# Linear attention and an MLP on one core: two more parts of GEMM 2 as seven products, and a new planned order of all instructions

## The chip, the cores and the metric

The kernel runs on one core of one Trainium2 chip. The metric is the device time of one execution in microseconds (us); three runs of the kernel before are shown as their median and their two ends. One further execution was taken by the hardware profiler. Its engines are named as the profile names them: PE (TensorE, matrix products), PEld (PE's loads of the stationary operand), DVE (VectorE), ACT (ScalarE), POOL (GpSimd) and SP (SyncE, which here issues nearly all DMA transfers).

## What is computed

```python
# q, k, v: (8, 8, 576, 64); omega: (128, 64); w_in: (512, 2048); w_out: (2048, 512)
def phi(x):                         # x already divided by 64 ** 0.25
    proj = einsum('bhsd,md->bhsm', x, omega)
    h = proj - sum(x * x, -1, keepdims=True) / 2
    return exp(h - max(h, -1, keepdims=True)) / sqrt(128)
kv = einsum('bhsm,bhsd->bhmd', phi(k), v);  z = sum(phi(k), axis=2)
x = einsum('bhsm,bhmd->bhsd', phi(q), kv) / (einsum('bhsm,bhm->bhs', phi(q), z) + 1e-6)
x = x.transpose(0, 2, 1, 3).reshape(4608, 512)
h = x @ w_in                        # GEMM 1
g = h * erf(softplus(h))
out = g @ w_out                     # GEMM 2
```

## The kernel before, in words

**Attention.** The 64 pairs of batch and head are worked off as 32 pairs of heads (`attention`, numbered 0_0 to 7_3 by batch and pair of heads). A pair goes through PE five times: `ppk` and `ppq` project keys and queries, `kvp` makes keys times values, `pt` turns the query features, and `nd` makes numerator and denominator. Between these steps DVE takes maxima, ACT takes exponentials and logarithms, and DVE divides (`xs`).

**The MLP.** The 4608 tokens are six groups: two of 2 x 288 tokens (groups 0 and 1), then four of 2 x 432 (`SUPERS`). The 2048 hidden features are four parts q of 512. Per group and part, GEMM 1 fills `hs`, `chain` applies softplus, erf and the product with h (`gs`, then `hs` again), and GEMM 2 adds the part into the output tiles `os`. All numbers are split into a high and a low part in a reduced format (names that end in h and l: `xh`, `xl`, `gh`, `gl`, `bh`, `bl`, `th`, `tl`; for weights both parts lie in a tile `w` or `wb`), and each product of two tiles takes three matmuls: high by high, high by low, low by high.

**Eight products or seven.** In the plain form (`plain1`, `gemm2`) a 2 x 2 block of tiles takes eight products. In the other form (`gemm1`, `gemm2_blocks`, by the table `PRODUCTS`, Winograd's variant of Strassen's method) it takes seven, on sums of weight blocks (made by `make_sums`: tiles `R`, then `S`, then their split `c`, stored to DRAM as `wdc` and fetched again as `wb`) and on sums of the right side (`xc` for GEMM 1, `gsum` in `pieces2` for GEMM 2). In the profile, matmuls of the plain form write tiles `h` and `o`; those of the seven products write `hX`, `hY`, `hZ` and `oX`, `oY`, `oZ`. `blocked(b, q)` decides for GEMM 2: with `FIRST2 = (3, 3, 3, 3)` groups 0 to 2 are plain in all four parts, groups 3 to 5 are in seven products, but for the very last part. The sums of a part's W2 are made where group `FIRST2[q] - 1` reads its plain weights, so all in group 2. GEMM 1 is in seven products from group 2 on; its sums (W1) are made in group 1. For a group of 432 and one part, GEMM 2 takes 4 output tiles x 2 halves x 4 x 3 = 96 matmuls in the plain form and 2 x 7 x 2 x 3 = 84 in the other.

**What sets the order.** `build` writes down operations with tiles they read and write, a due time (`plan`), and the engines that may do each, with a cost (`COST`, tuples such as `("V", 0.68, -1e9)`). `Plan.order` then plays the list through once on the host: due times are pulled forward along dependences, and at each step an idle engine takes the operation with the earliest due time whose inputs and buffers are there (`LAG` after the producer's end). What comes out is one fixed order per engine; on the chip every engine works off its own list in that order and waits on semaphores. `AHEAD` is how long before its due time a weight fetch may be issued by SP. Buffers are slots per pool (`SLOTS`: 8 for weights, 11 for the `g` pool that holds `hs`, `gs`, `gh`, `gl`, `R` and `S`, 8 PSUM banks) with limits per stream (`CAPS`: one `R` and one `S` at a time). All instructions are issued through one helper, so the profile shows one line, L1008, for nearly all of them, and groups are told apart by tiles.

Of the kernel before, what the change touches and what calls it, by code (L numbers as in the profile page):

```python
# [20 lines left out]
B, H, S, D = 8, 8, 576, 64  # L21
# [41 lines left out]
            ("Y", "S4", "B22", (0, 1), 1),  # L63
            ("X", "A22", "T4", (1, 0), 0))

FIRST2 = (3, 3, 3, 3)


def blocked(b, q):

    return FIRST2[q] <= b < len(SUPERS) - (q == NQ - 1)


COST = dict(mm=0.132, proj=0.222, half=0.156, tr=0.109, kv=1.35, table=1.3)
BANDWIDTH = 270e3
LAG = {"T": 0.35, "A": 0.25, "V": 0.25, "G": 0.3, "S": 0.3}
SLOTS = dict(w=8, g=11, u=2, f=2, mx=3, sq=3, v=1, qh=1, ql=1, kh=1, kl=1, xs=12, xh=2, xl=2,
             os=4, ps=8)
CAPS = dict(st=3, wt=1, ws=1, wp=2, cv=2, att=4, moe1=5, moe2=3, hs=4, gs=2, w=6, wsums=7)
# [26 lines left out]
class Plan:  # L106
# [43 lines left out]
    def order(self, slots, caps):  # L150
        ops = self.ops
# [5 lines left out]
        for o in reversed(ops):  # L157
            due = o.plan if o.plan is not None else math.inf
            dur = min(c for _, c, _ in o.opts)
            for s in o.succ:  # L160
                due = min(due, s.due - dur - 0.4)
            o.due = due
        free = {p: list(range(n)) for p, n in slots.items()}
        held = {s: 0 for s in self.streams}
        nxt = {s: 0 for s in self.streams}
# [16 lines left out]
        def event(t, kind, x):  # L182
            nonlocal count
            count += 1
            heapq.heappush(events, (t, count, kind, x))
# [22 lines left out]
        while True:  # L208
            progress = True
            while progress:  # L210
                progress = False
                for e in engines:
# [3 lines left out]
                    while ready[e]:  # L216
                        item = heapq.heappop(ready[e])
                        o = item[2]
# [22 lines left out]
                    o = chosen  # L241
# [41 lines left out]
            while True:  # L283
                if kind == "idle":
                    idle[x] = True
                elif kind == "done":
                    for s in x.succ:
                        s.left -= 1
                        lag = 0.0 if x.eng != "S" and len(s.opts) == 1 and s.opts[0][0] == x.eng \
                            else LAG[x.eng]  # L290
                        s.ready = max(getattr(s, "ready", 0.0) if s.left >= 0 else 0.0, now + lag) \
                            if hasattr(s, "ready") else now + lag
                        if not s.left:
                            event(max(now, s.ready), "push", s)
                    event(now + LAG[x.eng], "free", x)
                elif kind == "free":
# [19 lines left out]
    return n < WHOLE or WHOLE2[0] <= n < WHOLE2[1]  # L316


AHEAD = 40.0

SPANS = ((0, 288), (288, 288))

# [30 lines left out]
def build(emit):  # L353
# [49 lines left out]
    def fetch(u, t, src, ks, n):  # L403
        pl.op("wfetch", [("S", 0.1, AHEAD)], lambda e: E.fetch(t.ap[:, ks[0]:ks[-1] + 1].bitcast(F32), src()),
              reads=[(stored[u], 0)], writes=[(t, (x, k)) for x in "hl" for k in ks],
              size=P * n * BW * 8)
# [17 lines left out]
    def make(u, t):  # L424

        nm = "_".join(str(c) for c in u)
        st = pl.tile("w", f"st{nm}", [P, HW, 2], I32, "st")
        pl.op("wload", [("S", 0.1, AHEAD)], lambda e: E.w_load(st, u),
              writes=[(st, "h"), (st, "l"), (t, "room")], size=P * HW * 8)
# [9 lines left out]
    def room():  # L439
        count[0] += 1  # L440
        if clock[0] < starts[SUMS]:
            return CAPS["w"]
        return CAPS["wsums"] if clock[0] < starts[max(SUMS + 1, *FIRST2)] else SLOTS["w"]

# [61 lines left out]
    def weights2(ph, et, h):  # L506
        return unit(("2", ph, et, h))
# [390 lines left out]
    def gemm2(b, q, et):  # L898
# [16 lines left out]
        def one(t, f):  # L915
            if not ops:
                ops.extend(pl.tile("ps", f"o{b}_{q}_{et}_{i}", [P, 512], F32, "moe2",
                                   6 if b == len(SUPERS) - 1 else None) for i in range(2))
                w.append(weights2(q // 2, et, q % 2))
                if b == FIRST2[q] - 1:  # L920
                    beside[q, et] = w[0]
# [448 lines left out]
```

## Time and profile before

| what | value |
|---|---|
| median of three runs | 1030.14 us (1030.12 to 1030.81) |
| the profiled execution | 1036.67 us |
| its span, first to last instruction | 1034.9 us |
| mean granted TensorE clock | 0.993 of full speed |
| PE busy | 1006.5 us (97% of the span), 7132 instructions |
| DVE / ACT / POOL busy | 795.1 us (77%) / 683.7 us (66%) / 628.5 us (61%) |
| DMA | 232.72 MB, mean 225 GB/s |

Busy time is the union of an engine's instructions; PE's is pipelined, so single matmuls overlap and their mean length is longer than the distance from one to the next. A row of a group gives busy time and the mean of one instruction, then idle time before them with what ended it. The table by stretches gives busy time per engine in each stretch, with the granted clock and the share of the DMA engines. The profiled execution took 6.5 us longer than the median of the runs.

### The profile page before, as it was taken

How to read it: one execution, taken by the hardware profiler on the slowest of the kernel's cores; microseconds unless marked ns; L12 is line 12 of the kernel's file. 1: busy time of each engine (PE TensorE's matmuls, PEld its weight loads, DVE VectorE, ACT ScalarE, POOL GpSimd, SP SyncE). 2: the span in 40 equal slices, each digit the busy share in tenths (PEclk: the TensorE clock that was granted, in tenths of full speed). 3: DMA queues.
4: the chain of work that ended last, by engine and by line, in shares of the span. 5: the costliest groups of instructions: out<-in, count | busy, mean ns of one | idle time of the engine just before them, and what ended most of it. 6: DMA issues, size and time to landing. Idle time of an engine off the chain costs nothing.

```text
span 1034.9 us, 19457 instructions
## 1 busy us (share of the span) xinstructions
PE 1006.5 (97%) x7132; PEld 932.1 (90%) x7132; DVE 795.1 (77%) x1288; ACT 683.7 (66%) x1285; POOL 628.5 (61%) x467
## 2 busy tenths in 40 slices
PE   7999999999999899999999999999999999999998
PEld 6899889988999699999989899989899999999997
DVE  4888978897877747657787786889887788778664
ACT  7879887785676656855757575767658565645550
POOL 3435544875677728636876847569765388687520
PEclk9999998999999999999999999999999999999999
DMA  8276777597777467766547876666687546686651
GB/s 218 83 239 221 277 270 249 191 365 278 252 246 240 149 233 242 237 229 220 189 163 252 286 247 222 224 227 221 215 278 236 192 166 220 225 291 220 229 183 69
DMA packets 99486, 232.72 MB, mean 225 GB/s; under 512 B 11200, under 2 KB 11712, under 8 KB 99392
## 3 DMA queue, kind: packets, MB, share of 16 engines
q1 hardware_dynamic: 99232, 231.42, 67.1%
q8 instruction: 57, 0.93, 0.4%
q14 instruction: 37, 0.30, 0.1%
q10 hardware_dynamic: 160, 0.07, 0.0%
HBM read 188.45 MB, written 42.99 MB: 224 GB/s over the span
## 4 chain that ended last, share of the span: by engine, by line
PE 83%; DVE 8%; ACT 4%; DMA 3%; issue 2%; SPq 1%; ACTq 0%; DVEq 0%
PE o L1008 16%; PE hX L1008 14%; PE oX L1008 9%; PE h L1008 8%; PE hY L1008 7%; PE nd L1008 6%; PE oY L1008 5%; PE ppq L1008 4%; PE hZ L1008 4%; PE kvp L1008 3%; PE ppk L1008 3%; PE oZ L1008 2%; PE pt L1008 2%; DMA w<-wdw 1%; ACT L1008 1%
## 5 line engine op out<-in xcount | busy, mean ns | idle before, releaser
L1008 PE MATMUL o<-gh,w 128*128 128x288 f32 (+1 forms) x832 | 211.1, 329 | 0.6 <-DVE w L1008 0.6
L1008 PE MATMUL hX<-xh,wb 128*128 128x432 f32 x512 | 166.1, 370 | 2.3 <-DVE hs L1008 1.3
L1008 POOL TENSOR_TENSOR hs<-gs,hs 128x864 f32<-128x864 f32 (+1 forms) x44 | 97.6, 2242 | 101.0 <-ACT gs L1008 93.7
L1008 PEld LDWEIGHTS o<-gh,w 128*128 128x128 f32 x832 | 144.6, 188 | 6.1 <-DVE w L1008 1.1
L1008 PE MATMUL o<-gl,w 128*128 128x288 f32 (+1 forms) x416 | 132.7, 319 | 0.1
L1008 PE MATMUL h<-xh,w 128*128 128x288 f32 x512 | 126.0, 317 | 4.4 <-DVE w L1008 1.8
L1008 PEld LDWEIGHTS hX<-xh,wb 128*128 128x128 f32 x512 | 96.2, 188 | 9.1 <-DVE hs L1008 1.9
L1008 ACT ACT_TABLE_LOAD x75 | 96.2, 1283 | 2.1 <-PEq L1361 0.7
L1008 PEld LDWEIGHTS h<-xh,w 128*128 128x128 f32 x512 | 88.4, 193 | 9.4 <-DVE w L1008 2.5
L1008 PE MATMUL hX<-xl,wb 128*128 128x432 f32 x256 | 91.6, 358 | 0.0
L1008 ACT ACTIVATE fq<-ppq,mxq 128x128 f32<-128x128 f32 x288 | 78.6, 388 | 16.7 <-DVE mxq L1008 16.0
L1008 ACT ACTIVATE fk<-ppk,mxk 128x128 f32<-128x128 f32 x288 | 82.2, 380 | 9.7 <-DVE mxk L1008 9.3
L1008 ACT ACTIVATE hs<-hX 128x432 f32<-128x432 f32 x70 | 37.3, 532 | 74.6 <-PE hX L1008 73.8
L1008 PE MATMUL nd<-qh,kh 128*128 128x288 f32 x256 | 79.6, 417 | 7.2 <-ACT qh L1008 2.7
L1008 PE MATMUL hY<-xh,wb 128*128 128x432 f32 x256 | 84.0, 369 | 0.0
L1008 PE MATMUL oX<-th,wb 128*128 128x432 f32 x264 | 83.8, 367 | 0.0
L1008 ACT ACTIVATE rc<-nd,eps 64x288 f32<-64x288 f32 x128 | 63.6, 497 | 29.1 <-PE nd L1008 25.9
L1008 PEld LDWEIGHTS o<-gl,w 128*128 128x128 f32 x416 | 78.3, 188 | 2.9 <-DVE gl L1008 0.4
L1008 POOL TENSOR_TENSOR uq<-uq 128x288 f32<-128x288 f32 (+1 forms) x46 | 39.9, 888 | 67.2 <-PE h L1008 15.0
L1008 PE MATMUL h<-xl,w 128*128 128x288 f32 x256 | 76.7, 300 | 0.0
L1008 POOL TENSOR_TENSOR uk<-uk 128x288 f32<-128x288 f32 (+1 forms) x52 | 44.9, 884 | 51.1 <-DMA uk<-kT 23.4
L1008 DVE TENSOR_TENSOR xs<-nd,rc 64x288 f32<-64x288 f32 (+1 forms) x160 | 62.9, 393 | 14.9 <-ACT rc L1008 11.7
(142 smaller groups left out, 2700.2 us busy)
## 6 DMA issues: line engine op xcount, KB each, us to landing
wb<-wdc SPq DMA_DIRECT2D x216, 256.0 KB, 3.5
wb<-wdw SPq DMA_DIRECT2D x162, 256.0 KB, 3.8
w<-wdw SPq DMA_DIRECT2D x52, 512.0 KB, 4.5
st<-w SPq DMA_DIRECT2D x32, 512.0 KB, 5.0
wdw<-w SPq DMA_DIRECT2D x32, 512.0 KB, 4.4
wdc<-c SPq DMA_DIRECT2D x32, 512.0 KB, 4.8
v<-vP SPq DMA_DIRECT2D x32, 325.0 KB, 4.6
uk<-kR SPq DMA_DIRECT2D x24, 320.0 KB, 3.7
```

What stands on the lines that cost most here:

```text
L1008: return tc.keep_in_program_order(method(*args, **kwargs))
```

## The change

Four things are edited.

- `FIRST2` becomes `(3, 3, 2, 2)`: in group 2 (the third group of tokens) parts 2 and 3 of GEMM 2 are done in seven products, and the sums of W2 for these two parts are made in group 1 instead of group 2.
- The five `LAG` numbers and `AHEAD` change slightly.
- A table `JITTER` of 25 windows of due time is added. In `order`, after due times are known, every operation whose due time lies in a window gets a fixed pseudo-random shift of up to the window's amplitude (0.5 to 8 us; six of the windows have amplitude zero). No instruction is added by this: it changes who comes first where two operations compete.

```diff
-FIRST2 = (3, 3, 3, 3)
+FIRST2 = (3, 3, 2, 2)
...
-LAG = {"T": 0.35, "A": 0.25, "V": 0.25, "G": 0.3, "S": 0.3}
+LAG = {"T": 0.3402, "A": 0.2525, "V": 0.2605, "G": 0.3153, "S": 0.2979}
...
             o.due = due
+        for k, (lo, hi, amp) in enumerate(JITTER):
+            for o in ops:
+                if lo <= o.due < hi:
+                    o.due += amp * ((o.id * 7919 + k * 104729 + 17) % 1009 / 504.0 - 1.0)
         free = {p: list(range(n)) for p, n in slots.items()}
...
-AHEAD = 40.0
+JITTER = ((0, 0, 0), (186.1, 206.1, 4), (0, 0, 0), (0, 0, 0), (0, 0, 0), (227.5, 727.5, 4),
...
+AHEAD = 39.82
```

Counted over the whole program, PE loses 192 matmuls into `o` (128 with `gh`, 64 with `gl`) and gains 168 into `oX`, `oY` and `oZ`. SP issues 16 more fetches of `wb` from `wdc` and 12 more from `wdw` (256 KB each), and 8 fewer of `w` from `wdw` (512 KB each). The additions into `os` on DVE, ACT and their copies grow by 12.

The order changes nearly everywhere. Three places matter below. In the names, `nd_3_3_0_1` is batch 3, pair 3, head 0, second half; `o1_2_0_1` is group 1, part 2, output tile 0, half 1; `hX2_0_0` is group 2; `h111_1_3` is the plain form of group 1.

**PE where group 2 begins.** Before, the last two attention steps of batch 3 and the first ones of batch 4 follow each other, with no matmul of the MLP between:

```order
L1008 MATMUL hX2_0_1_4602<-xh2_0_4335,wb63_4345 128x432
L1008 MATMUL pt_3_3_2_4673<-ident_67,fq_3_3_4583 128x128 x3
L1008 MATMUL nd_3_3_0_0_4682<-qh_3_3_4636,kh_3_3_4592 128x288
L1008 MATMUL nd_3_3_1_0_4686<-qh_3_3_4636,kh_3_3_4592 128x288
L1008 MATMUL nd_3_3_0_1_4690<-qh_3_3_4636,kh_3_3_4592 128x288
L1008 MATMUL nd_3_3_1_1_4701<-qh_3_3_4636,kh_3_3_4592 128x288
L1008 MATMUL ppq_4_0_0_4707<-wr_71,uq_4_0_4570 128x128
...
L1008 MATMUL ppq_4_0_1_4726<-wr_71,uq_4_0_4570 128x128
L1008 MATMUL kvp_4_0_4729<-v_4_0_4588,fk_4_0_4668 64x2x65 x2
L1008 MATMUL kvp_4_0_4729<-v_4_0_4588,fk_4_0_4668 64x65 x16
L1008 MATMUL hZ2_0_0_4768<-xh2_0_4335,wb64_4407 128x432
```

Now the same steps stand earlier, with matmuls of group 1 between them (30 in all between `pt_3_3_2` and `kvp_4_0`, where there were none), and group 2 begins after them:

```order
L1017 MATMUL pt_3_3_2_4485<-ident_67,fq_3_3_4379 128x128 x3
L1017 MATMUL o1_2_0_1_4464<-gh1_5_4150,w2_1_0_0_57_4063 128x288
...
L1017 MATMUL o1_2_0_0_4434<-gh1_5_4150,w2_1_0_0_57_4063 128x288
L1017 MATMUL nd_3_3_0_0_4517<-qh_3_3_4440,kh_3_3_4354 128x288
L1017 MATMUL nd_3_3_1_0_4521<-qh_3_3_4440,kh_3_3_4354 128x288
L1017 MATMUL nd_3_3_0_1_4525<-qh_3_3_4440,kh_3_3_4354 128x288
L1017 MATMUL o1_2_2_0_4530<-gh1_4_4143,w2_1_2_0_58_4105 128x288
...
L1017 MATMUL nd_3_3_1_1_4535<-qh_3_3_4440,kh_3_3_4354 128x288
...
L1017 MATMUL o1_2_1_0_4558<-gh1_4_4143,w2_1_1_0_59_4279 128x288
L1017 MATMUL ppq_4_0_0_4567<-wr_71,uq_4_0_4344 128x128
...
L1017 MATMUL kvp_4_0_4587<-v_4_0_4357,fk_4_0_4480 64x2x65 x2
L1017 MATMUL hX2_0_0_4683<-xh2_0_4461,wb61_4370 128x432
```

So pair 3_3 moved ahead of three quarters of GEMM 2's part 2 of group 1 (72 of its 96 matmuls): between `nd_3_3_0_1` and the first product of group 2 on a sum (`hY2`) there are now these 72 matmuls into `o1_2` and 12 into `hX2`; before, that first `hY2` stood 17 instructions ahead of it.

**SP at the same place.** `w2_1_0_1` to `w2_1_3_1` are W2 for part 3 of group 1, `wb72` on are blocks of W1 for group 2, and `uk_4_2` are keys of pair 4_2. Before:

```order
L1008 DMA uk_4_1_4633<-kN 128x576
L1008 DMA w2_1_0_1_68_4652<-wdw2_1_0_1_33_2691 128x1024
L1008 DMA uq_4_1_4748<-qR 128x640
L1008 DMA w2_1_2_1_69_4810<-wdw2_1_2_1_34_2788 128x1024
L1008 DMA w2_1_1_1_70_4820<-wdw2_1_1_1_35_2857 128x1024
L1008 DMA w2_1_3_1_71_4826<-wdw2_1_3_1_36_2941 128x1024
L1008 DMA wb72_4852<-wdw1_0_4_5_872 128x512
L1008 DMA wb72_4852<-wdw1_0_6_7_1017 128x512
L1008 DMA uk_4_2_4864<-kR 128x640
L1008 DMA uk_4_2_4864<-kN 128x576
L1008 DMA wb73_4875<-wdc1_0_2_1_3152 128x512
```

Now, with the stores of the sums of W2 (`wdc2_2_...`, which wait until POOL, DVE or ACT have written `c2_2_...`) between them:

```order
L1017 DMA wdc2_2_0_0_4794<-c2_2_0_0_4770 128x1024
L1017 DMA w2_1_0_1_68_4806<-wdw2_1_0_1_33_2711 128x1024
L1017 DMA w2_1_2_1_69_4831<-wdw2_1_2_1_34_2789 128x1024
L1017 DMA w2_1_1_1_70_4847<-wdw2_1_1_1_35_2929 128x1024
L1017 DMA w2_1_3_1_71_4853<-wdw2_1_3_1_36_2974 128x1024
L1017 DMA uk_4_2_4861<-kR 128x640
L1017 DMA wb72_4868<-wdw1_0_4_5_857 128x512
L1017 DMA wdc2_2_0_1_4874<-c2_2_0_1_4845 128x1024
L1017 DMA wb72_4868<-wdw1_0_6_7_1002 128x512
L1017 DMA uk_4_2_4861<-kN 128x576
L1017 DMA wdc2_2_1_0_4945<-c2_2_1_0_4910 128x1024
L1017 DMA wb73_4956<-wdc1_0_2_1_3222 128x512
```

The first of the eight stores for parts 2 and 3 moved from row 290 of SP's list to row 201, the last from 356 to 245.

**DVE at the end.** The gate of the last part (`hs5_1_2`, `hs5_1_3`) and its low parts (`gl5_6`, `gl5_7`), on which the last plain GEMM 2 waits, before:

```order
L1008 TENSOR_TENSOR os5_0_10782<-oZ5_2_0_11390,os5_0_10782 128x432
L1008 TENSOR_TENSOR hs5_1_2_11210<-gs5_6_11343,hs5_1_2_11210 128x1728
L1008 TENSOR_TENSOR hs5_1_3_11234<-gs5_7_11344,hs5_1_3_11234 128x1728
L1008 TENSOR_TENSOR os5_1_10791<-oZ5_2_1_11412,os5_1_10791 128x432
L1008 TENSOR_TENSOR os5_2_10803<-oX5_2_0_11333,os5_2_10803 128x432
L1008 TENSOR_TENSOR gl5_6_11441<-hs5_1_2_11210,gh5_6_11423 128x1728
L1008 TENSOR_TENSOR os5_3_10812<-oX5_2_1_11346,os5_3_10812 128x432
L1008 TENSOR_TENSOR gl5_7_11454<-hs5_1_3_11234,gh5_7_11435 128x1728
```

And now:

```order
L1017 TENSOR_TENSOR os5_0_10809<-oZ5_2_0_11423,os5_0_10809 128x432
L1017 TENSOR_TENSOR hs5_1_2_11249<-gs5_6_11386,hs5_1_2_11249 128x1728
L1017 TENSOR_TENSOR os5_1_10820<-oZ5_2_1_11443,os5_1_10820 128x432
L1017 TENSOR_TENSOR hs5_1_3_11259<-gs5_7_11387,hs5_1_3_11259 128x1728
L1017 TENSOR_TENSOR gl5_6_11478<-hs5_1_2_11249,gh5_6_11463 128x1728
L1017 TENSOR_TENSOR os5_2_10830<-oX5_2_0_11361,os5_2_10830 128x432
L1017 TENSOR_TENSOR gl5_7_11487<-hs5_1_3_11259,gh5_7_11480 128x1728
```

So one addition into `os` stands between the first gate and `gl5_6`, where there were two, and it stands before the second gate. On PE, 78 matmuls stood between the last one of GEMM 1 and the first one of the last part of GEMM 2; now there are 72.

4 rows, old and new, of the table JITTER are left out of this document.

## Prediction

> **What bounds the kernel now.** I read the page first, then the table by stretches, then PE's own rows and the chain of waits where PE stands still.
>
> ```profile
> span 1034.9 us, 19457 instructions
> PE 1006.5 (97%) x7132; PEld 932.1 (90%) x7132; DVE 795.1 (77%) x1288; ACT 683.7 (66%) x1285; POOL 628.5 (61%) x467
> ```
>
> PE is busy for all but 28 us. So time can be saved in three ways only: fewer matmuls, less idle time of PE, or fewer stretches in which PE runs at a lower clock. The next table gives length, busy time of each engine, granted clock, DMA share and rate for each stretch.
>
> ```profile
> core 0: us, PE busy (x) PEld busy (x) DVE busy (x) ACT busy (x) POOL busy (x), PEclk, DMA share, GB/s
> 46.00:152.00 106.00, 101.19 (x846) 95.50 (x845) 90.69 (x167) 87.41 (x170) 48.83 (x42) 1.00 0.71 247
> 152.00:200.00 48.00, 45.97 (x353) 43.10 (x354) 41.59 (x74) 36.35 (x77) 29.84 (x29) 0.93 0.66 233
> 200.00:346.00 146.00, 143.78 (x1294) 134.46 (x1292) 114.44 (x211) 100.83 (x221) 102.07 (x102) 1.00 0.77 262
> 346.00:366.00 20.00, 14.80 (x118) 12.01 (x119) 15.48 (x28) 13.78 (x39) 12.82 (x12) 0.91 0.56 186
> 366.00:435.00 69.00, 69.00 (x485) 64.18 (x485) 44.60 (x72) 47.01 (x77) 33.85 (x25) 1.00 0.69 231
> 435.00:520.00 85.00, 85.00 (x506) 78.95 (x507) 59.47 (x98) 52.80 (x91) 54.22 (x39) 1.00 0.64 212
> 520.00:610.00 90.00, 88.65 (x648) 80.07 (x647) 69.41 (x121) 59.08 (x124) 56.33 (x45) 1.00 0.74 252
> 610.00:800.00 190.00, 189.50 (x1308) 172.14 (x1307) 157.57 (x254) 131.52 (x254) 137.51 (x87) 1.00 0.69 227
> 800.00:995.00 195.00, 194.00 (x1042) 183.46 (x1041) 154.63 (x181) 106.41 (x131) 132.81 (x67) 1.00 0.66 220
> 995.00:1035.00 40.00, 35.55 (x180) 33.32 (x178) 20.11 (x26) 12.74 (x9) 0.00 (x0) 1.00 0.29 103
> ```
>
> Two stretches stand out. In 346 to 366, where group 2 begins, PE idles 20.00 - 14.80 = 5.2 us, and a granted clock of 0.91 means that 0.09 x 20 = 1.8 us more are lost: 7.0 us in all. In 152 to 200 it is 2.0 us of idle time and 0.07 x 48 = 3.4 us of clock: 5.4 us. From 366 to 995, by contrast, PE idles only 1.35 + 0.5 + 1.0 = 2.85 us in 629 us. This is PE in 346 to 366 where it stood still (in brackets the idle time before, and what ended it):
>
> ```profile
> 352.88 1.80 PE L1008 MATMUL nd<-qh,kh 128*128 128x288 f32 x6 [0.52 <-ACT fk L1008]
> 355.92 0.75 PE L1008 MATMUL nd<-qh,kh 128*128 128x288 f32 x2 [1.24 <-DVE xs L1008]
> 360.02 0.80 PE L1008 MATMUL ppq<-wr,uq 128*128 128x128 f32 x2 [2.26 <-DVE xs L1008]
> 363.73 0.46 PE L1008 MATMUL hZ<-xh,wb 128*128 128x432 f32 x1 [0.55 <-ACT kh L1008]
> ```
>
> And the chain of waits there, after a run of plain matmuls:
>
> ```profile
> 333.94 8.45 PE o L1008 x64
> ...
> 351.69 2.18 ACT fk L1008 x8
> ...
> 355.90 0.46 DVE xs L1008
> ...
> 357.99 1.50 DVE xc L1008
> ...
> 360.82 2.39 PE kvp L1008 x36
> ```
>
> It goes through ACT and DVE, because the attention steps of pairs 3_3 and 4_0 follow each other on PE with no other matmul between them.
>
> **The change part by part.**
>
> *Fewer matmuls.* Two parts of group 2 go from 96 to 84 matmuls, so 24 of 432 columns go. Their distance comes from the last run of such matmuls, in the chain of the end:
>
> ```profile
> 1005.61 1.95 DVE hs L1008
> 1007.57 1.03 DVE os L1008 x2
> 1008.60 1.88 DVE gl L1008
> 1010.52 1.25 PE o L1008 x5
> ...
> 1012.94 17.71 PE o L1008 x90
> ```
>
> 17.71 / 90 = 0.197 us, and 24 x 0.197 = 4.7 us. These parts stand in 435 to 610, where PE idles 1.35 us in 175, so this counts whole: **-4.7 us**. It would be given back only if the new form starves PE. Groups 3 to 5 already work in that form, and there PE idles 1.5 us in the 385 us from 610 to 995.
>
> *The start of group 2.* In the new order 30 matmuls stand between `pt_3_3_2` and `kvp_4_0`, and between the `nd` that group 2 needs and its first product on a sum (`hY2`) there are 72 matmuls at 8.45 / 64 = 0.132 us and 12 at 0.197: 9.5 + 2.4 = 11.9 us of cover. The chain above takes from 355.90 (first division) to 363.73, 7.8 us. It fits. What is late next: `nd` still follows the last `pt` closely, with 12 matmuls (1.6 us) between. A stall of that kind is priced by these rows of PE:
>
> ```profile
> 152.10 0.55 PE L1008 MATMUL pt<-ident,fq 128*128 128x128 f32 x3 [0.49 <-DVE qh L1008]
> 153.47 0.75 PE L1008 MATMUL nd<-qh,kh 128*128 128x288 f32 x2 [0.82 <-ACT qh L1008]
> 155.03 0.61 PE L1008 MATMUL h<-xh,w 128*128 128x288 f32 x1 [0.81 <-ACT w L1008]
> 156.18 0.85 PE L1008 MATMUL h<-xh,w 128*128 128x288 f32 x2 [0.31 <-DVE w L1008]
> ```
>
> The first two make 0.49 + 0.82 = 1.3 us, which I leave in. So 7.0 - 1.3: **-5.7 us** (ends: 0 if the stall only moves, -7.0 if all goes).
>
> About the clock, row first: the longest single idle time in 346 to 366 is 2.26 us, in 152 to 157 it is 0.82 us, and yet both stretches lost clock. [...]
>
> *The sums of W2, moved.* Four sets of sums go from group 2's parts 2 and 3 to the end of group 1. What 16 sets cost:
>
> ```profile
> L1008 POOL TENSOR_TENSOR R<-w 128x512 f32<-128x512 f32 x16 | 21.4, 1343 | 5.2 <-DMA w<-wdw 5.2
> L1008 DVE TENSOR_TENSOR R<-w 128x512 f32<-128x512 f32 x16 | 16.7, 1046 | 2.3 <-DMA w<-wdw 2.3
> 0.00:1035.00 1035.00, 20.11 (x30) 4.42 (x7) 81.10 (x91) 0.99 0.68 225
> ```
>
> The last row is the table by stretches for tile `S` alone (DVE, ACT, POOL). 21.4 + 16.7 + 105.6 = 143.7 us, or 9.0 per set and 36 for four. They now fall into 346 to 435, beside the sums for parts 0 and 1. DVE, ACT and POOL together idled 29 + 28 + 42 = 99 us there (89 us less 60.1, 60.8 and 46.7 busy), so they fit; if that cover were gone, a third of 36, 12 us, would reach PE. The eight stores of 512 KB add 4.2 MB to 89 us, 47 GB/s on top of 186 to 231; 262 GB/s ran in 200 to 346 with PE at 98%. I take **0**.
>
> *More side work for two parts in seven products.* Sums and splits of `gs`, 12 more additions into `os`, 28 more fetches for 8 fewer. They lie in 435 to 610 too, where DVE idles 175 - 128.9 = 46 us, and groups 3 to 5 carry the same load. **0**.
>
> *The end.* 78 matmuls now 72: 6 x 0.197 = 1.2 us less cover for the last gate, and one addition (1.03 / 2 = 0.5) less ahead of `gl5_6`. PE already came just in time there (0.25 us late at 1010.52), so **+0.6 us** (ends 0 and +1.2).
>
> *The shifted order elsewhere.* Nearly every list changes, while up to 157 PE's order is almost the same. I take **0**, with ends of -5.4 (the loss in 152 to 200 goes) and +5.4 (one more such place).
>
> Sum: -4.7 - 5.7 + 0.6 = -9.8 us. The profiled execution took 1036.67 us, of which 1.8 lie outside its span, and is 6.5 above the median of the runs; stalls and matmuls are the same in both, so I take the difference from the median: 1030.1 - 9.8 = **1020.3 us**.
>
> **The rivals.** A measurement of this kernel can tell about 0.2%, 2.1 us, from no change.
>
> *The stall only moves* to another place where attention steps follow each other: 1030.1 - 4.7 + 0.6 = 1026.0. For it: the whole order is new, and five attention steps per pair must go somewhere. Against: in 366 to 520, with attention between MLP matmuls throughout, PE did not idle at all.
>
> *The loss in 152 to 200 goes too*: 1020.3 - 5.4 = 1014.9. For it: its stalls are 0.3 to 0.8 us, and only together did they cost clock. Against: PE's order there hardly differs, and DVE and ACT are at 86% and 82% up to it.
>
> *SP holds back the weights, and the kernel gets slower.* SP now waits for `c2_2` and `c2_3` with W1 blocks of group 2 (`wb72` on) and keys of 4_2 queued behind. Waits of SP for these stores before (total, times, longest), and how far ahead blocks come:
>
> ```profile
> SPq L1008 <- DVE c L1008: 20.1, 8, 4.8
> SPq L1008 <- POOL c L1008: 14.2, 8, 2.9
> ```
>
> ```profile
> 333.31 6.74 SPq L1008 DMA_DIRECT2D wb<-wdc  x4
> ```
>
> ```profile
> 349.76 0.36 PE L1008 MATMUL hY<-xh,wb 128*128 128x432 f32 x1
> ```
>
> 34.3 / 16 = 2.1 us per store, 17 for eight; the lead is 349.76 - 340.05 = 9.7 us. If the slips add up with no recovery, 7.4 us of stall result, still faster (1027.7). It decides above (9.7 + 9.8) / 8 = 2.4 us each: at 3.0, within the longest, 24 - 9.7 = 14.3 us give 1034.6. Against: the 16 stores of W2's sums stood between block fetches before, and PE idled 1.35 us from 366 to 610.
>
> *It gives nothing*: the products go, but two new places like 152 to 200 take 10 us back: about 1030.
>
> **How the numbers follow.** Forecast 0.55, stall moves 0.20, deeper gain 0.12, no change 0.07, SP 0.06. The forecast's own range is 1018.4 (all 7.0 us go, nothing is lost at the end) to 1023.8 (half of the 5.7 stays, 1.2 at the end). The range for 8 in 10 reaches down through the deeper gain and the 2.4 us of idle time in 520 to 610 and 800 to 995 (1012.5), and up past the moved stall by 2 us (1028.0). Faster by over 0.2% are the first three, 0.86 after what the second may lose; within 0.2% 0.08; slower 0.06.
>
> **What would show it.** Right: PE has 24 fewer matmuls, and near the start of group 2 a granted clock of 1.00 and idle time under 1.5 us. Wrong: a stretch after 157 with PE idle for over 2 us or a clock under 0.95, SP's waits for `c` above 2.4 us each, or more than 1.5 us before the last part of GEMM 2.

## Result and profile after

| | median | runs |
|---|---|---|
| before | 1030.99 us | 10, 1030.12 to 1033.2 |
| after | 1042.87 us | 10, 1033.61 to 1048.09 |

The change makes the kernel slower: ratio 1.0104, interval 1.0075 to 1.0132. The runs of the changed kernel also lie much further apart, 14.5 us against 3.1. Its profiled execution took 1045.04 us, with a granted clock of 0.990. The head of its page:

```profile
span 1043.2 us, 19463 instructions
PE 1005.1 (96%) x7108; PEld 931.2 (89%) x7108; DVE 814.7 (78%) x1305; ACT 703.1 (67%) x1300; POOL 634.8 (61%) x466
```

The 24 matmuls are gone (7132 to 7108). Taken at full clock, PE's busy time is about 1005.1 - 0.010 x 1043.2 = 994.7 us, against 1006.5 - 0.007 x 1034.9 = 999.3 before: 4.6 us less. But PE idles 1043.2 - 1005.1 = 38.1 us instead of 28.4, and runs at half clock for 21.3 us of its span instead of 13.7. The table by stretches shows where:

```profile
core 0: us, PE busy (x) PEld busy (x) DVE busy (x) ACT busy (x) POOL busy (x), PEclk, DMA share, GB/s
46.00:152.00 106.00, 100.75 (x843) 96.01 (x841) 89.79 (x158) 86.04 (x167) 45.40 (x37) 0.98 0.72 243
...
200.00:346.00 146.00, 141.22 (x1281) 131.06 (x1280) 115.28 (x220) 106.66 (x245) 95.76 (x89) 1.00 0.77 262
346.00:366.00 20.00, 20.00 (x130) 19.13 (x130) 17.27 (x26) 14.69 (x22) 17.87 (x14) 1.00 0.62 216
366.00:435.00 69.00, 69.00 (x487) 64.35 (x486) 53.43 (x90) 48.68 (x80) 44.54 (x39) 1.00 0.78 263
435.00:520.00 85.00, 80.43 (x500) 74.38 (x499) 68.73 (x94) 54.08 (x93) 64.77 (x49) 0.98 0.72 248
520.00:610.00 90.00, 88.94 (x611) 79.86 (x610) 70.17 (x125) 61.46 (x119) 51.60 (x37) 0.98 0.69 227
610.00:800.00 190.00, 184.63 (x1271) 166.65 (x1271) 153.67 (x246) 129.71 (x248) 119.19 (x78) 0.99 0.66 220
800.00:995.00 195.00, 190.61 (x1014) 179.59 (x1013) 149.51 (x177) 112.21 (x131) 136.43 (x69) 0.99 0.65 214
```

The start of group 2 (346 to 366) has no loss left: no idle time, clock 1.00. The price stands in places that were nearly free before: 4.6 us of idle time in 435 to 520 (0 before), 5.4 in 610 to 800 (0.5), 4.4 in 800 to 995 (1.0), 4.8 in 200 to 346 (2.2). The longest single stalls in PE's rows, with what ended each (left out is one of 3.8 us near the start, which the kernel before has too, with 3.9):

```profile
113.45 0.40 PE L1017 MATMUL h<-xh,w 128*128 128x288 f32 x1 [2.19 <-DVE w L1017]
...
220.90 0.40 PE L1017 MATMUL h<-xh,w 128*128 128x288 f32 x1 [2.51 <-ACT kh L1017]
...
518.74 0.70 PE L1017 MATMUL hX<-xh,wb 128*128 128x432 f32 x1 [4.57 <-issue]
...
684.12 0.73 PE L1017 MATMUL hZ<-xh,wb 128*128 128x432 f32 x1 [4.20 <-DVE xs L1017]
...
959.96 0.47 PE L1017 MATMUL hX<-xh,wb 128*128 128x432 f32 x1 [3.07 <-DVE hs L1017]
```

The stall at 514 is put down to nothing visible. But PE goes on 0.11 us behind DVE's copy into `kh` (518.16 + 0.47 = 518.63), and that copy stands on DVE behind the subtraction that makes `xl3_1`, which PE multiplies soon after. DVE's and POOL's rows of the timeline show how late that was:

```profile
508.73 0.75 DVE L1017 TENSOR_REDUCE sk<-uk 128x9 f32<-128x576 f32 x1
509.39 8.85 DVE L1017 TENSOR_TENSOR xl<-xs,xh 128x432 fp32r<-128x432 f32 x1
518.16 0.47 DVE L1017 COPY kh<-kvp 128x128 f32<-128x128 f32 x2
...
508.51 1.29 POOL L1017 TENSOR_TENSOR uq<-uq 128x288 f32<-128x288 f32 x2
509.76 8.01 POOL L1017 TENSOR_TENSOR hs<-gs,hs 128x864 f32<-128x864 f32 x4
```

The kernel cuts POOL's larger operations in two, and such pieces follow each other without a gap; in a row that says x4, four pieces stand together. DVE's subtraction lasts 8.85 us, from just before four POOL pieces to 0.47 us behind the last of them (517.77). At 675.54 the cast `th3_2_0` takes 6.23 us in the same way, beside two pieces of `bb` and two of `bl`; the stall at 680 follows:

```profile
675.54 6.23 DVE L1017 CAST th<-gs 128x1728 fp32r<-128x1728 f32 x1
...
674.69 2.18 POOL L1017 TENSOR_TENSOR bb<-hs,bb 128x432 fp32r<-128x432 f32 x2
676.83 4.01 POOL L1017 TENSOR_TENSOR bl<-hs,bh 128x864 fp32r<-128x864 f32 x2
```

The theory to test was therefore **holds**: a DVE operation that meets POOL's pieces usually gets in at the next border between two pieces, but sometimes misses it and is held until POOL's whole row is through. The rival is that **the order itself** makes PE wait, in every execution alike.

### The profile page after: what moved, and what is told of

The parts are those of the page before. It is cut to its first block, busy times and chain, and to the rows that moved or that the text cites. A ratio compares the mean times of both kernels' runs of the same rounds, so it can differ in the third digit from the quotient of the medians.

```text
span 1043.2 us, 19463 instructions
## 1 busy us (share of the span) xinstructions
PE 1005.1 (96%) x7108; PEld 931.2 (89%) x7108; DVE 814.7 (78%) x1305; ACT 703.1 (67%) x1300; POOL 634.8 (61%) x466
## 4 chain that ended last, share of the span: by engine, by line
PE 77%; DVE 12%; ACT 4%; issue 4%; POOL 2%; DMA 1%; SPq 1%; POOLq 0%; DVEq 0%; ACTq 0%
PE hX L1017 13%; PE o L1017 12%; PE oX L1017 10%; PE h L1017 9%; PE hY L1017 6%; PE nd L1017 5%; PE oY L1017 5%; PE ppq L1017 4%; PE kvp L1017 3%; PE hZ L1017 3%; PE ppk L1017 3%; PE oZ L1017 3%; DVE hs L1017 2%; PE pt L1017 2%; DVE gs L1017 2%
## 5 line engine op out<-in xcount | busy, mean ns | idle before, releaser
L1017 POOL TENSOR_TENSOR hs<-gs,hs 128x864 f32<-128x864 f32 (+1 forms) x50 | 111.8, 2259 | 107.7 <-ACT gs L1017 104.7
L1017 PE MATMUL o<-gh,w 128*128 128x288 f32 (+1 forms) x704 | 170.1, 320 | 0.4 <-DVE w L1017 0.2
L1017 PEld LDWEIGHTS o<-gh,w 128*128 128x128 f32 x704 | 120.5, 188 | 4.5 <-DVE w L1017 0.6
L1017 PE MATMUL o<-gl,w 128*128 128x288 f32 (+1 forms) x352 | 109.8, 312 | 0.8 <-DVE gl L1017 0.8
L1017 PE MATMUL oX<-th,wb 128*128 128x432 f32 x312 | 101.6, 368 | 0.7 <-DVE os L1017 0.7
L1017 POOL TENSOR_TENSOR uq<-uq 128x288 f32<-128x288 f32 (+1 forms) x46 | 45.3, 1003 | 62.1 <-DMA uq<-qN 27.5
L1017 POOL TENSOR_TENSOR tl<-gs,th 128x864 fp32r<-128x864 f32 x32 | 68.4, 2160 | 15.8 <-ACT th L1017 6.9
L1017 ACT ACTIVATE qh<-pt 128x384 f32<-128x384 f32 x53 | 25.6, 492 | 71.4 <-PE pt L1017 71.4
L1017 DVE TENSOR_TENSOR os<-oX,os 128x432 f32<-128x432 f32 x86 | 51.2, 603 | 24.7 <-PE oX L1017 24.2
L1017 ACT ACTIVATE gs<-hs 128x1728 f32<-128x1728 f32 (+1 forms) x48 | 69.5, 1481 | 0.3
```

Source lines behind the costliest of these rows:

```text
L1017: return tc.keep_in_program_order(method(*args, **kwargs))
```

## The experiments

All ratios are against runs of the kernel before in the same batch, with the 95% interval.

**The two edits apart.** e1 and e2 each make one half of the change:

```diff
 # e1: the kernel before
-FIRST2 = (3, 3, 3, 3)
+FIRST2 = (3, 3, 2, 2)
 # e2: the changed kernel
-FIRST2 = (3, 3, 2, 2)
+FIRST2 = (3, 3, 3, 3)
```

> The kernel before with FIRST2 = (3, 3, 2, 2) alone: the seven products and the earlier sums of W2, but the old LAG, AHEAD and no JITTER. PE has 24 matmuls fewer than before, up to 346 its order is that of before. If the products and sums themselves are what costs (more DVE and POOL work in 435 to 610 and around the start of group 2), it is as slow as the changed kernel, 1038 to 1046 us, with PE stalls of over 2 us in 435 to 610. If the cost comes from places that a given order happens to make (DVE work behind a row of POOL pieces, PE with little in hand), this order has others: 1020 to 1036 us, the stalls at 514, 680 and 957 are not there, and the loss in 152 to 200 stays as before.

> The changed kernel with FIRST2 = (3, 3, 3, 3): the new LAG, AHEAD and JITTER alone, eight products and the sums of W2 where they were before. The order up to 346 is that of the changed kernel, later it is a third one. If the products cost, it is at 1025 to 1032 us. If each order has its own chance places, 1028 to 1045, with the stalls at 111 and 218 (order up to 346, the same) as in the changed kernel and others than at 514, 680 and 957 behind; and its single runs spread by over 5 us where those of before spread by 3.

Measured: e1 1034.35 us (1029.96 to 1037.31), ratio 1.0009 (0.999 to 1.0027); e2 1041.05 us (1037.18 to 1044.16), ratio 1.007 (1.0046 to 1.0095). Most of the loss comes from the new numbers of the planner, without a single new product. But the seven products gain nothing either, though they save 24 matmuls here too. e1's profile has a hold of its own (a `tl` of 6.15 us at 534.56); e2's, taken in the fastest of its seven executions, has none. Against what was expected, e1 does not keep the lost clock around 152: from 140 to 200 its clock is 1.00 (0.94 before), with about the same idle time (2.8 us against 2.4).

**What recurs.** e3 and e4 profile the unchanged program twice more.

> The changed kernel unchanged, another profile, for what recurs. If the order itself makes the stalls (ACT or DVE busy with something else when PE needs them), all of those at 111, 218, 514, 680 and 957 recur with the same length within 0.3 us. [...]

> The same kernel once more, a third profile, as for the second.

Measured: 1052.23 us and 1029.54 us, one program. In e3 both holds recur (8.85 and 6.22 us). In e4 neither does. Its head and the rows at the first place:

```profile
span 1027.8 us, 19463 instructions
PE 998.1 (97%) x7108; PEld 925.7 (90%) x7108; DVE 804.6 (78%) x1305; ACT 704.1 (69%) x1300; POOL 637.6 (62%) x466
```

```profile
505.61 0.75 DVE L1017 TENSOR_REDUCE sk<-uk 128x9 f32<-128x576 f32 x1
506.27 0.86 DVE L1017 TENSOR_TENSOR xl<-xs,xh 128x432 fp32r<-128x432 f32 x1
...
505.37 1.30 POOL L1017 TENSOR_TENSOR uq<-uq 128x288 f32<-128x288 f32 x2
506.62 6.16 POOL L1017 TENSOR_TENSOR hs<-gs,hs 128x864 f32<-128x864 f32 x2
```

The same operation, the same row of POOL pieces, and 0.86 us. DVE began 0.90 us behind POOL's first `uq` piece (506.27 - 505.37), against 0.88 in the first profile and 0.89 in e3 (516.33 - 515.44), both held: 0.01 to 0.02 us separate the two outcomes. The stalls at 111 (2.21 us in e4), 218 (2.51) and 957 (3.02) are there in all three profiles, so those belong to the order. Both theories are borne out, for different stalls.

**Memsets between the pieces.** e5 puts a 128x1 memset on POOL between the pieces of the two rows, e6 behind every POOL operation; e7 cuts POOL's gates, rests and differences in four instead of two; e8 is e6 on the kernel before.

```diff
+            def call(*args, **kwargs):
+                r = method(*args, **kwargs)
+                if next(calls) in (269, 270, 271, 272, 273, 336, 337, 338, 339):   # e5
+                    tc.keep_in_program_order(self.engine.memset(gap, 0.0))
+                return r
 # e7, in gate, rest and less_halves
             for i in halves(e, 2):
+                for c in halves(e, gs.ap.shape[-1]):
```

> The changed kernel with nine tiny memsets (128x1) on POOL, between the pieces of two rows: gate hs_1_2, hs_1_3 (where xl3_1 on DVE took 8.85 us in two of three profiles) and bb_2, bl_2 (where th3_2_0 took 6.23). They make no work for anybody else. [...]

> The changed kernel with a tiny memset (128x1) behind every one of POOL's 460 operations. [...] If the order is to blame, as the changed kernel: 1038 to 1048.

> The changed kernel with POOL's gates, rests and differences in four pieces instead of two, the order of everything else the same. If a normal wait of DVE is for the rest of one piece (up to 2.0 us), the excess of DVE's operations falls from 73 to 84 us in all to 40 to 55, and the stalls at 957 (3.07 us) and 583 (1.06) shrink by about 1 and 0.5 us. A missed hand-over still costs the whole row of pieces, so where it happens it stays as long (8 us at 514). [...] Time 1026 to 1046.

> The kernel before with the same memsets behind every POOL operation. [...] If the memsets by themselves cost (POOL's time), it is slower, 1034 to 1040.

Measured: e5 1033.98 us (1032.46 to 1035.64), ratio 1.0028 (1.0015 to 1.0041); e6 1036.13 us (1032.72 to 1039.82), 1.0044 (1.0026 to 1.0062); e7 1035.6 us and e8 1030.21 us, one run each. Nine memsets of 0.1 us, which add work and take none away, bring the changed kernel from a ratio of 1.0104 to 1.0028 (1042.87 to 1033.98 us). The rows in e5:

```profile
507.52 0.92 DVE L1018 TENSOR_TENSOR xl<-xs,xh 128x432 fp32r<-128x432 f32 x1
...
507.90 0.11 POOL L1035 MEMSET gap<- 128x1 f32 x1
507.95 2.42 POOL L1018 TENSOR_TENSOR hs<-gs,hs 128x864 f32<-128x864 f32 x1
```

`xl3_1` takes 0.92 us and PE does not idle in the 20 us around it. e6 shows that holds are not all: its profile has none, and it is still slower than the kernel before, at a ratio of 1.0044. e7 tells a single wait from a hold. DVE's busy time, which includes its waiting, falls to 787.5 us from 804.6 in e4: with shorter pieces the normal waits are shorter. But a missed border costs the whole row, however it is cut. In e7 the cast `th3_2_0` meets eight pieces:

```profile
666.87 7.57 DVE L1017 CAST th<-gs 128x1728 fp32r<-128x1728 f32 x1 [0.55 <-POOL gs L1017]
...
666.80 2.46 POOL L1017 TENSOR_TENSOR bb<-hs,bb 128x216 fp32r<-128x216 f32 x4
669.23 4.29 POOL L1017 TENSOR_TENSOR bl<-hs,bh 128x432 fp32r<-128x432 f32 x4
```

It lasts 7.57 us, and PE idles 5.83 us behind it. The stall at 957 shrank less than expected (3.07 to 2.68 us), and the one at 583 grew (1.06 to 2.37), where another DVE operation, `gs3_1`, took 5.31 us.

**Moves in the order.** e9 adds four moves to e5, and two memsets at a third row (`bb`, `tl` at 583, where `gs3_1` is held for one piece in every profile of the changed kernel and in e5's). e10 has the moves and no memset.

```diff
+MOVES = (((1129,), 1202),             # kh_2_2 ahead of a weight step and a softplus (218)
+         ((599,), 587), ((600,), 588),  # w1_1_2 ahead of w1_1_1 (111)
+         ((4551, 4558), 4557),        # a sum that waits for POOL behind two copies of hX5_1 (944)
+         ((3350, 3351), 3300))        # two divisions ahead of a sum (671)
```

> The changed kernel with the nine memsets, two more between the last pieces of bb and tl at 583 (the hold that was left), and four moves in the fixed order: kh_2_2 on ACT ahead of a weight step and a softplus (stall of 2.51 us at 218); on DVE the join and the high part of w1_1_2 ahead of those of w1_1_1, since PE takes w1_1_2 first (2.19 at 111); two divisions that free PSUM ahead of a sum of gates (1.95 at 671); two copies of hX5_1 out of PSUM ahead of a sum that waits for POOL (3.02 at 944). If what keeps the changed kernel from its gain, once the holds are gone, is the order in these places, the four stalls shrink to under 0.6 us each, PE's idle time falls from 21 to 11 to 13 us, and the time from 1034.0 to 1023 to 1027 us, faster than the kernel before by 0.4 to 0.8%. If PE waits for work that is late whatever the order (DVE and ACT have too much), the idle time comes back elsewhere: 1031 to 1035.

> The same four moves without any memset, so the other half of the two by two. If holds and order are two separate losses, the moves alone gain about the same 7 to 9 us against the changed kernel, 1033 to 1037 us, and the runs keep their spread of over 8 us, since whether POOL's rows hold DVE is still chance. If the holds came only from the old order of DVE, no hold over 4 us and as fast as with the memsets.

Measured: e9 1029.68 us (1027.84 to 1032.22), ratio 0.9977 (0.9965 to 0.9989), faster than both kernels, though less than expected. e10 1042.66 us (1041.75 to 1043.6), ratio 1.0096 (1.0074 to 1.0119): as slow as the changed kernel, against my expectation of 1033 to 1037; its profile has both holds, and its four runs lie 1.9 us apart and not over 8. So, from e5 to e9, the moves are worth 4 to 5 us without the holds (1033.98 to 1029.68, or 1.0028 to 0.9977), and nothing that can be seen with them. The two memsets that e9 has besides did not remove the hold beside them: `gs3_1` takes 4.10 us. The stall at 671 (680 in the first profile) shrinks from 1.95 to 0.5 us and the one at 944 (957) from 3.0 to 1.5. At 111 and 218 the wait did not shrink, it only changed its name:

```profile
112.90 0.40 PE L1020 MATMUL h<-xh,w 128*128 128x288 f32 x1 [1.16 <-DVE w L1020]
114.56 0.40 PE L1020 MATMUL h<-xh,w 128*128 128x288 f32 x1 [1.13 <-DVE w L1020]
...
222.31 0.40 PE L1020 MATMUL o<-gh,w 128*128 128x288 f32 x1 [1.59 <-DVE w L1020]
...
228.30 0.40 PE L1020 MATMUL o<-gh,w 128*128 128x288 f32 x1 [2.08 <-ACT w L1020]
```

There PE waits for prepared weights (`w`), whichever comes first. Behind 218 stand ACT's rows of the changed kernel:

```profile
214.93 1.17 ACT L1017 ACTIVATE gs<-hs 128x1152 f32<-128x1152 f32 x1
216.12 1.28 ACT L1017 ACT_TABLE_LOAD   x1
217.41 0.63 ACT L1017 ACTIVATE wt<-st 128x512 f32<-128x512 f32 x1
218.06 1.28 ACT L1017 ACT_TABLE_LOAD   x1
219.35 1.16 ACT L1017 ACTIVATE gs<-hs 128x1152 f32<-128x1152 f32 x1
220.42 0.42 ACT L1017 ACTIVATE kh<-kvp 128x128 f32<-128x128 f32 x2
```

The weight step `wt` between two softplus costs two table loads, 2.56 us. In `build` it carries no `set`, so the planner charges nothing for that.

**Both edits without holds.** e11 is e1, e12 is e2 and e13 the kernel before, each with the memsets of e6; e14 is the changed kernel, timed again.

> Seven products for two more parts and the sums of W2 sooner, in the order that the old numbers give, with a tiny memset behind every POOL operation. Its profile without them had one DVE operation held over four POOL pieces (6.15 us, a stall of 1.69 at 542). If the seven products pay once nothing is held, 1026 to 1031 us, below the kernel before with the same memsets; if they bring as much waiting as the 24 matmuls save (4.7 us), 1031 to 1035.

> Eight products as before, in the order that the new numbers (lags, jitter, reach of fetches) give, with a memset behind every POOL operation. If the 9 us that this order alone costs are holds, 1030 to 1034 us; if they are its fixed stalls (2.19 at 112, 2.51 at 219, 2.37 at 886) and the clock behind them, 1036 to 1041 as without memsets.

> The kernel before with a memset behind every POOL operation, timed: what the memsets cost by themselves. 1030 to 1033 us if nothing, 1034 or more if POOL's 5 to 28 us more of work reach PE.

> The changed kernel unchanged, timed on the same chip as these: 1038 to 1045 us in the median, single runs from 1029 to 1052; runs without the holds at 514 and 680 (clock 0.995 and more) below 1036, runs with them above 1038.

Measured, with ratio and interval:

| | old numbers | new numbers |
|---|---|---|
| eight products | before | e2 1041.05, 1.007 (1.0046 to 1.0095) |
| seven | e1 1034.35, 1.0009 (0.999 to 1.0027) | e14 1043.42, 1.0116 (1.0099 to 1.0133) |
| eight, memsets | e13 1029.21, 0.998 (0.9971 to 0.9989) | e12 1036.28, 1.0041 (1.0025 to 1.0056) |
| seven, memsets | e11 1032.84, 1.0012 (1.0003 to 1.0022) | e6 1036.13, 1.0044 (1.0026 to 1.0062) |

The memsets by themselves add 17.3 us to POOL's busy time (645.8 us in e8's profile, 628.5 before) and nothing to the time of the kernel before (e13). With memsets everywhere the new numbers cost 7.1 us with eight products and 3.3 with seven, and the seven products cost 3.6 us in the old order and nothing in the new one. In no combination do they gain. e12, which was to fall to 1034 us or less if the new numbers cost by holds, stayed at 1036, where fixed stalls were to leave it. e14's profiled execution (1044.45 us) has the hold of `xl3_1` (8.84 us) and not that of `th3_2_0` (1.18). PE's rows of e11 at the start of group 2 show one reason in the old order:

```profile
350.74 0.55 PE L1008 MATMUL pt<-ident,fq 128*128 128x128 f32 x3 [1.68 <-DVE qh L1008]
352.68 3.25 PE L1008 MATMUL nd<-qh,kh 128*128 128x288 f32 x6 [0.91 <-DVE qh L1008]
362.86 1.35 PE L1008 MATMUL kvp<-v,fk 128*64 128x130 f32 x16 [2.92 <-DVE hs L1008]
```

The sums do not remove the stall there, they make it longer. The same stretch in e11, in e13 and in e2:

```profile
346.00:366.00 20.00, 13.86 (x98) 10.54 (x97) 16.89 (x31) 11.62 (x29) 17.28 (x29) 0.73 0.61 201
346.00:366.00 20.00, 15.17 (x102) 12.60 (x101) 11.76 (x21) 12.17 (x32) 10.68 (x20) 0.83 0.38 127
346.00:366.00 20.00, 20.00 (x156) 19.28 (x152) 18.53 (x25) 14.81 (x23) 16.40 (x11) 1.00 0.77 246
```

With old numbers PE idles 6.1 us with the sums (e11) and 4.8 without (e13), and the clock is lower too. With new numbers and eight products (e2) it doesn't idle at all: it is the new numbers that cleared the place. Later, from 435 to 800, e11's PE idles 4.3 us and e13's 0.7; one of e11's stalls there, 1.36 us at 719, is put down to a memset.

## Why the prediction was wrong

- **Fewer matmuls, -4.7 us: right.** 24 fewer, and 4.6 us less busy time at full clock.
- **The start of group 2, -5.7 us: right in place and kind, a little small.** 346 to 366 lost all its 7.0 us, more than the 5.7 I took. As I read from the lists, the new order does it: e2 has it without the seven products, and with the old numbers the stall stays (e1, e11).
- **The sums of W2, moved, 0: right in the new order, wrong in the old one** (e11 above). In the changed kernel PE is busy for all 89 us from 346 to 435. SP's wait for the stores did rise, as I named for the rival and the wrong sign: 45.2 us for 17 waits, 2.7 each, above the 2.4 at which it was to decide. No idle time follows there, so no cost of it shows.

```profile
SPq L1017 <- DVE c L1017: 37.4, 13, 8.5
...
SPq L1017 <- POOL c L1017: 7.8, 4, 5.9
```

- **The end, +0.6 us: right in size.** The first matmul on `gl` starts 1.12 us behind the one before it (at 1018.08), against 0.45 before (1010.52 - 1010.07): 0.67 us more.

```profile
1019.20 0.46 PE L1017 MATMUL o<-gl,w 128*128 128x432 f32 x1 [0.76 <-DVE gl L1017]
```

- **More side work for two parts in seven products, 0 ("DVE idles 46 us"): wrong.** An engine's idle time in a stretch is no cover. e13 and e11 differ by this edit and its sums alone: 3.6 us slower while 4.7 us of matmuls go, so about 8 us of waits and clock came with them in the old order (5.6 by e1, without memsets). In the new order e12 and e6 take the same time, so there about 5 us came with them.
- **The shifted order elsewhere, 0, with ends of -5.4 and +5.4: wrong, and the step that failed.** e2 has this term and the start of group 2 together: 0.7% slower, 7.2 us, although it wins the start of group 2 in full. So the order elsewhere cost about 7.2 + 7.0 = 14 us by itself, against the 0, with an end of 5.4, that I took. What the changed kernel shows has two parts. The fixed stalls stand in all profiles of it: about 2.2 us at 111, 2.5 at 218, 1.9 at 680 and 3.0 at 957, so four new places instead of "one more" (the stalls at 150 to 155, the longest of 1.3, add up to 2.5 us, as they did before). The holds add 4.57 us of idle time at 514 and 2.3 at 680 (4.20 less the 1.91 that e4 has there), and clock behind each (0.83 in the 20 us from 505, 0.89 in the 15 us from 675, 1.00 at both in e4). I had seen neither the mechanism nor that a new order draws new places for it.
- **Taking the difference from the median, because "stalls and matmuls are the same in both": loose, but not what failed.** The profiled execution of before ran at clock 0.993, most others at 0.995 to 0.998, so 2 to 5 us of its lost clock were not in the median. Two other profiles of that order (e8 and e13, with memsets) put it elsewhere: from 140 to 200 they idle as long as the profile of before (2.5 and 2.7 us against 2.4), but at clocks of 0.97 and 1.00 and not 0.94, while in 346 to 366 they still idle 4.9 and 4.8 us, at 0.91 and 0.83.

From the sum to the result: 1020.3 forecast, 1042.9 measured, 22.6 us apart. The ratios split this in two. The new numbers (e2) were to give -5.7 us and cost 7.2: 12.9 apart. The seven products with their sums, on top of these numbers, were to give -4.7 + 0.6 = -4.1 and cost 3.5 (1.0104 less 1.0070): 7.6 apart. Of the other 2.1, 0.9 is that the kernel before took 1030.99 in ten runs and 1030.14 in three; the rest is within the intervals. Cut the other way, the two holds are about 8 of the 20.5, by e5 (1.0104 less 1.0028), and 12 to 13 are left for the fixed stalls, the waits that came with the seven products, and the clock behind both; the four moves win back 4 to 5 of these. How much each of those parts takes is not settled. Of the rivals, "it gives nothing", with two new places, was the nearest in kind; the one given for slower, SP, shows no part.

Not settled: what decides whether DVE misses a border. At `xl3_1` DVE began 0.88 to 0.90 us behind POOL's first `uq` piece in the four profiles where it was held (the first, e3, e10 and e14), and 0.90 in e4, where it was not: the rows do not tell the two apart. In e6 and e11, with a memset behind every POOL operation, no DVE operation was held, while the profiles of the same orders without them have one to three holds. But the memsets did not help at the third row of e9. Whether they work by the gap or by shifting times was not told apart. Why e2, whose profile has no hold, falls from 1.0070 to 1.0041 with them (e12) is open, as the profile is one execution. Why they make the kernel before 0.2% faster (e13), whose profile has no hold either, is open too.

## What to carry to other kernels

An order that is fixed by replaying a planner needs more than one timed run and more than one profile: the changed program took 1029.5 us in one execution and 1052.2 in another, and a replay that charges DVE the rest of POOL's current piece, as `Plan.order` does, sees neither. Look at rows of several POOL pieces without a gap beside a DVE operation that PE needs soon; break such a row with something tiny (cutting its pieces finer did not help), or give PE work in hand there, which was not tried here. Do not cover added side work with an engine's idle share of a long stretch: ask at each place which operation PE waits for next.

## What the runs showed of the hardware

**A wait for POOL has two sizes.** In the four profiles of the changed kernel (its own, e3, e4 and e14) 466 operations of DVE beside POOL's took at least 0.1 us longer than the quickest tenth of their kind. 457 of them took at most 1.9 us longer, less than one piece of 2.0 us. The 9 others took 3.0 to 8.3 us longer: DVE was held past one to four borders (in e7 past seven), and got in only when POOL had no further piece for about 3 us or more (3.0, 3.3 and 10.1 us in the first profile, which has 3 of the 9). Beside the held operation at 509 POOL's four pieces keep 2.0 us each (8.01 / 4), while in e4, where DVE gets in between, the first two take 6.16 us.

**The same stall may cost clock or not.** Behind the stall at 111 the clock fell to half in the first profile:

```profile
108.00:114.00 6.00, 3.80 (x31) 3.33 (x29) 5.97 (x11) 5.40 (x11) 3.77 (x3) 1.00 0.69 259
114.00:117.40 3.40, 3.22 (x14) 3.22 (x15) 3.40 (x7) 1.52 (x3) 3.40 (x4) 0.50 0.75 290
```

and in e4, after 2.21 us instead of 2.19, it did not:

```profile
113.00:117.00 4.00, 3.67 (x24) 3.33 (x25) 3.97 (x7) 2.19 (x5) 4.00 (x4) 1.00 0.71 278
```

The stretch lasts 3.4 us and costs 1.7. In the first profile every stretch at half clock, but for the one at the very end, lasts 3.41 or 6.83 us, and they begin whole multiples of 3.41 us apart (at 114.0, 155.0, 516.8, 684.1 and 960.5). The profile of before shows the same two lengths (at 18.4, 154.9 and 359.7). So the length of a stall did not decide here whether clock was lost: 2.19 us cost 1.7 more in one execution, 2.21 us cost none in another. An estimate from these two, for this kernel: a stall of 2 us is to be priced as 2 us and a chance of 1.7 more.
